# A decode step of attention: values as the 512-wide moving operand in six groups in place of two, and output weights on the lowest eight DMA engines

## The chip, the cores and the metric

The kernel runs on one core of a Trainium2 chip. A core has TensorE (matrix products, written to PSUM), VectorE, ScalarE, GpSimdE and SyncE, and 16 DMA engines that carry data from HBM to SBUF, the on-chip memory of 128 partitions. The engines run on their own and meet at semaphores. The metric is the device time of the kernel in microseconds; the profile's span is that of one profiled execution, from its first to its last instruction.

## What is computed

One token goes through attention with 32 heads of 128 values over the last 4096 positions of a cache, beside a small gated network; the two are multiplied and added to the input. Cut to what matters:

```python
xn = layernorm(A_x)                                  # 1 x 512
q  = (xn @ A_wq).reshape(32, 128)
k, v = A_k_cache[:, 32768-4096:], A_v_cache[:, 32768-4096:]      # per head 4096 x 128
p  = softmax(q @ k.T * 128**-0.5)                    # per head 1 x 4096
o  = (p @ v).reshape(1, 4096)                        # all heads side by side
s  = o @ A_wo                                        # 1 x 512
h  = gelu(layernorm(xn + mix(gelu(layernorm(xn) @ B_w1)) @ B_w2) @ B_w3) @ B_w4
out = A_x + s * silu(xn + mix(...) @ B_w2 + h)
```

With one position, the shifted mix of the small network is zero. K and V are 32 MB each of bf16, and each number is used once. The matrix w4 has 1376 rows (ten blocks of 128, and 96), wo has 4096 rows.

## The kernel before

**Groups and stages.** The 32 heads are worked in 8 groups of 4. A group's K is one tile of 128 partitions by 128 columns by 128 values (4 MB): each head has 32 partitions, and each column holds one position of each partition. V is the same. A loop of ten stages runs K two groups ahead of V (`LAG = 2`): stage s scores the keys of group s, takes the softmax of group s-1, and multiplies the values of group h = s-2. TensorE, VectorE and ScalarE work in exactly the written order (a manual schedule); a wait of one instruction holds all that is behind it on its engine.

**Scores.** Of the 128 columns, `nd(g)` go to VectorE, in four parts of a product and a sum (L308, L310): 64 columns in groups 0, 1 and 7, 68 in group 3, 80 in the others. The rest go to TensorE in batches of up to 8: a transpose (L324), a copy by ScalarE (L326), a product with q (L332). `keys(b0, b1)` does some of these batches.

**Softmax.** `sm_max` (VectorE) takes the maximum per partition, `sm_turn` turns it on TensorE (L354) and VectorE takes the maximum per head (L356), `sm_exp` spreads it (L363) and takes four exponentials on ScalarE (L370). `sm_den` (L376) adds up the sums, and `sm_rden` (L381) takes the reciprocal on VectorE.

**Values**, `v_part`. In the ordinary form (L430) each of the 128 columns of V is the stationary operand, and the four probabilities of the column are the moving one: 128 weight loads and 128 narrow products, which give the 4 heads as columns. In the form for groups in `MOVED` (L422) the probabilities of four columns are the stationary operand (16 wide), and four columns of V, 512 numbers, the moving one: 32 loads and 32 wide products, which give 16 by 512 numbers. Only the blocks where the two column numbers agree are wanted. ScalarE copies them to SBUF (L425), and `v_add` (L437) adds the four blocks with selected columns of the identity: 4 float32 products, which the machine runs as 8. `v_add` and `v_out` of a group in `MOVED` are in the next stage, behind `sm_den` and `sm_rden`; for the others `v_out` (L453, for the last two groups L449) follows at once. The results of `sm_den`, `v_add`, `sm_turn` and `sm_exp` share one PSUM buffer, so each waits until the one before it has been read.

**The output product.** wo is used in three blocks: heads 0 to 15 (`wo0`, by the wide product L496 in stage 6), heads 16 to 23 (stage 8), and heads 24 to 31. In the last, heads that finish early are spread to partitions by `ox_spread`, `ox_pick` and `ox_few`, so that one group of 32 small products covers several heads (`y_block`, L150), and the remaining ones go head by head (`y_head`). `NE` says over how many DMA engines this block's early rows, the tile `wo_few`, are laid out: `FEW = 64 * NE` rows. With `NE = 5` these are 320 rows, heads 24, 25 and half of 26. Its load has two parts, each with an outer dimension of `NE`. The other rows come as `wo_rows`: half of head 26 and head 27 ahead of the last V, heads 28 to 31 behind it.

**Loads.** SyncE issues all the big loads (L79) in one order, as written, each when its buffer is free: K has three buffers (one of them later holds wo), V has two. So V of a group is issued when the values two groups before are done. The last V comes in cuts of 64, 48 and 16 columns, and TensorE multiplies each as it lands.

Of the kernel before, what the change touches and what calls it, by code (L numbers as in the profile page):

```python
# [8 lines left out]
P = 128  # L9
# [9 lines left out]
G = 4  # L19
LAG = 2  # L20
K_BUFS = 3
NE = 5
V_BUFS = 2
EARLY = 2
LATE = 7
MOVED = (0, 2)


@with_exitstack
def kernel(  # L30
# [14 lines left out]
    nc = tc.nc  # L45
# [3 lines left out]
    _, H, Sk, Dh = A_k_cache.shape  # L49
# [8 lines left out]
    F = B_w3.shape[1]  # L58
# [19 lines left out]
    def load(dst, src):  # L78
        return tc.keep_in_program_order(nc.sync.dma_start(out=dst, in_=src))  # L79
# [9 lines left out]
    load(w3_sb[:], B_w3.rearrange("(p c) n -> p c n", p=P))  # L89
    w4_sb = wts.tile([P, 11, D], BF16, name="w4_sb")  # L90
    load(w4_sb[:, 0:10, :], B_w4[0:10 * P, :].rearrange("(p c) n -> p c n", p=P))
    load(w4_sb[0:96, 10, :], B_w4[10 * P:F, :])
    wq_sb = wts.tile([P, KC, HD], BF16, name="wq_sb")

    load(wq_sb[:].rearrange("p c n -> p (c n)"), A_wq.rearrange("(a b c) n -> b a (c n)", a=2, c=KC))
# [51 lines left out]
    def rows_add(ps, col, w, last):  # L147
        k = col.shape[0]
        for j in range(KC):
            nc.tensor.matmul(ps[32 * j:32 * j + 1, :], lhsT=col, rhs=w[0:k, j * P:(j + 1) * P],  # L150
                             start=False, stop=last, skip_group_check=True)
# [114 lines left out]
    for c in range(2):  # L266
        nc.vector.tensor_copy(
            out=few[:, c, 0:4 * NE].rearrange("p (a b) -> p a b", b=4),
            in_=ident_bf[:, 4 * NE * c:4 * NE * (c + 1)].rearrange("p (b a) -> p a b", b=4))

# [79 lines left out]
    def sm_turn(g):  # L350

        s = st[g]
        mt_ps = ps_misc.tile([1, P], FP32, tag="misc", name="mt_ps")
        nc.tensor.transpose(mt_ps[:], s["m1"][:], ident_f[:])  # L354
        mx = sm_pool.tile([1, G], FP32, tag="mx", name="mx")
        nc.vector.tensor_reduce(out=mx[:], in_=mt_ps[:].rearrange("r (b a) -> r a b", a=G), axis=AX.X,  # L356
                                op=ALU.max)
        nc.vector.tensor_scalar(out=md[0:1, :], in0=mx[:], scalar1=-scale, scalar2=None, op0=ALU.mult)
# [28 lines left out]
    few_h = blocks[few_block][0]  # L387
    FEW = 8 * 8 * NE
    h_part = few_h + FEW // P

    r_part = FEW % P
    o_blk, wo_blk, ox_blk = {}, {}, {}

    def load_wo(i):
        h0, n = blocks[i]
        load(wo_blk[i], A_wo[h0 * P:(h0 + n) * P, :].rearrange("(p t) n -> p t n", p=P))

    def load_few():
        t = wo_blk[few_block]
        for c in range(2):  # L400
            r0 = few_h * P + c * FEW // 2
            load(t[32 * c:32 * c + 4 * NE],
                 A_wo[r0:r0 + FEW // 2, :].rearrange("(b a t) n -> a b (t n)", b=4, a=NE))

    def wo_row(h):
        return wo_rows[:, h - h_part, :]

    def load_rows(h, n):
        if h == h_part:
            load(wo_rows[r_part:P, 0, :], A_wo[h * P + r_part:(h + 1) * P, :])  # L410
            h, n = h + 1, n - 1
        load(wo_rows[:, h - h_part:h - h_part + n, :],
             A_wo[h * P:(h + n) * P, :].rearrange("(h p) n -> p h n", p=P))

# [2 lines left out]
    def v_part(g, v, c0=0, c1=CP):  # L417
        s = st[g]
        if g in MOVED:
            s["ov"] = ps_o.tile([4 * G, 4, Dh], FP32, tag="oT", name="ov")  # L420
# [12 lines left out]
    def v_add(g):  # L433
        s = st[g]
        s["oT"] = ps_misc.tile([P, G], FP32, tag="misc", name="oT")
        for j in range(4):
            nc.tensor.matmul(s["oT"][:], lhsT=s["ov_sb"][:, j, :], rhs=ident_f[0:4 * G, G * j:G * j + G],  # L437
                             start=(j == 0), stop=(j == 3))

    def v_out(g):  # L440
        h = G * g
        b = [i for i, (h0, _) in enumerate(blocks) if h >= h0][-1]
        if b not in o_blk:
            o_blk[b] = sm_pool.tile([P, blocks[b][1]], BF16, tag=f"o{b}", bufs=1, name="o")
            if b == few_block:
                nc.gpsimd.memset(o_blk[b][:], 0.0)
        c = h - blocks[b][0]
        if g >= NG - 2:
            nc.vector.tensor_tensor(out=o_blk[b][:, c:c + G], in0=st[g]["oT"][:], in1=st[g]["rden"][:],  # L449
                                    op=ALU.mult)  # L450
            return
        for k in range(G):
            nc.scalar.mul(o_blk[b][:, c + k:c + k + 1], st[g]["oT"][:, k:k + 1], st[g]["rden"][:, k:k + 1])  # L453


    def ox_spread(i):
        n = blocks[i][1]
        to, mt, mh = masks[n]
        spread = sm_pool.tile([P, n, n], BF16, tag=f"spread{n}", bufs=1, name="spread")
        nc.vector.tensor_tensor(out=spread[:], in0=o_blk[i][:].unsqueeze(2).to_broadcast([P, n, n]),  # L460
                                in1=mt[:].unsqueeze(1).to_broadcast([P, n, n]), op=ALU.mult)
        ox_blk[i] = spread
# [42 lines left out]
    def y_head(h):  # L505
        rows_add(y_ps, o_blk[few_block][:, h - few_h:h - few_h + 1], wo_row(h), h == H - 1)
# [7 lines left out]
    for s in range(NG + LAG):  # L514
        h = s - LAG
        last = h == NG - 1
        kn = load_kv(k_pool, A_k_cache, s, (0, 64, CP) if s == 0 else (0, CP)) if s < NG else None
        if s == LAG:
            wts_guard.__exit__(None, None, None)
            v_pool = ctx.enter_context(tc.tile_pool(name="v", bufs=V_BUFS))  # L520
            wo_blk[few_block] = v_pool.tile([64, 8, D], BF16, tag="wo_few", bufs=1, name="wo_few")
            nc.gpsimd.memset(wo_blk[few_block][:], 0.0)
            wo_rows = v_pool.tile([P, H - h_part, D], BF16, tag="wo_rows", bufs=1, name="wo_rows")
            nc.gpsimd.memset(wo_rows[0:r_part, 0, :], 0.0)
        if last:
            load_rows(h_part, 2)
            v = load_kv(v_pool, A_v_cache, h, cuts)
            for r, n in ((H - G, 2), (H - 2, 1), (H - 1, 1)):
                load_rows(r, n)
        elif h >= 0:  # L530
            v = load_kv(v_pool, A_v_cache, h)
        if h == 3:
            wo_24 = k_pool.tile([P, 32, D], BF16, tag="kv", name="wo_24")
            wo_blk[0], wo_blk[1] = wo_24[:, 0:16, :], wo_24[:, 16:24, :]
            load_wo(0)
        if h == 5:
            load_wo(1)
            load_few()

        if s < NG:  # L540
            nb = len(batches(s))

            def keys(b0, b1):
                for b in range(b0, b1):
                    k_turn(s, kn, b)
                    if b > 0:
                        k_scores(s, b - 1)

            k_open(s)
            k_vector(s, kn, 0)  # L550
            keys(0, 2)
            if s > 1:
                sm_den(s - 2)
                sm_rden(s - 2)
            if h - 1 in MOVED:
                v_add(h - 1)
                v_out(h - 1)
            keys(2, 4)
            k_vector(s, kn, 1)
            if s > 0:  # L560
                sm_turn(s - 1)
            if s == 6:
                ox_spread(0)
            keys(4, nb)
            k_scores(s, nb - 1)
            sm_own(s)
            if s > 0:
                sm_exp(s - 1)
            k_vector(s, kn, 2)
            if s == 6:  # L570
                ox_pick(0)
            k_vector(s, kn, 3)
            if h >= 0:
                v_part(h, v)
            sm_max(s)
            if s == 6:
                y_wide(0, 0, 16)
            if h >= 0 and h not in MOVED:
                v_out(h)
        elif s == NG:  # L580

            sm_den(NG - 2)
            sm_rden(NG - 2)
            sm_turn(NG - 1)
            ox_spread(1)
            sm_exp(NG - 1)
            ox_pick(1)
            y_block(1)
            rows_add(y_ps, one_f, y_row, False)
            v_part(h, v)  # L590
            v_out(h)
            ox_spread(few_block)
            sm_den(NG - 1)
            sm_rden(NG - 1)
            ox_pick(few_block)
            ox_few(few_block)
        else:
            v_part(h, v, 0, cuts[1])
            y_block(few_block)
            for r in range(h_part, H - G):  # L600
                y_head(r)
            for c0, c1 in zip(cuts[1:], cuts[2:]):
                v_part(h, v, c0, c1)
            v_out(h)
            for r in range(H - G, H):
                y_head(r)
# [36 lines left out]
```

## Time and profile before

The median of three timed runs is 195.14 us (194.98 to 195.44), the profiled span 193.2 us.

| engine | busy us | share of the span |
|---|---|---|
| PE (TensorE products) | 132.6 | 69% |
| PEld (weight loads, beside the products) | 102.3 | 53% |
| DVE (VectorE) | 143.8 | 74% |
| ACT (ScalarE) | 87.1 | 45% |
| all loads | 78.84 MB read | mean 408 GB/s |

The page gives for each engine its busy share in 40 slices of the span (4.83 us each) as a digit in tenths, and below it the granted TensorE clock, the busy share of the DMA engines, and the rate. A timeline line has the start and the length in us, the engine, the line of the kernel, the operation, what is written and read, and how many instructions were merged; in brackets stands how long the engine was idle before, and what ended that. Where the reason is "issue", the engine waited for nothing that the profile shows.

### The profile page before, as it was taken

The numbers are of one execution on the slowest core, as the hardware profiler recorded it, in microseconds if no ns is written. First come the engines' busy times: TensorE is split into PE (matmuls) and PEld (weight loads), VectorE is DVE, ScalarE is ACT, GpSimd is POOL, SyncE is SP. The second block draws the span as 40 slices with busy tenths as digits, with TensorE's granted clock in tenths as the row PEclk, the third lists the DMA queues.
The fourth block names the chain that finished last, engine by engine and source line by source line (L and its number), as shares of the span: only waits on it lengthen the run. The fifth ranks groups of instructions, "written<-read, shape, count | busy, mean of one in ns | idle before, by whom it ended". The sixth has DMA issues, their size and how long they took to land.

```text
span 193.2 us, 4769 instructions
## 1 busy us (share of the span) xinstructions
PE 132.6 (69%) x2123; PEld 102.3 (53%) x2123; DVE 143.8 (74%) x162; ACT 87.1 (45%) x195; POOL 6.4 (3%) x14
## 2 busy tenths in 40 slices
PE   0549763977736579798898938840878879845792
PEld 0444463866625433486884428740768257733771
DVE  0560208999999999999999999990899999931201
ACT  2003002888896360468568044731574077813000
POOL 2110008000000000000000000000000000000000
PEclk9999955588755557978559995855576696755555
DMA  6999999999999999999999999999999999999980
GB/s 205 417 472 427 397 427 453 421 427 424 434 431 434 434 433 421 434 427 434 424 431 434 431 434 407 461 431 434 431 427 426 427 424 407 458 417 377 416 326 8
DMA packets 4725, 79.13 MB, mean 410 GB/s; under 512 B 666, under 2 KB 1466, under 8 KB 1722
## 3 DMA queue, kind: packets, MB, share of 16 engines
q1 hardware_dynamic: 4554, 78.84, 96.0%
q8 instruction: 16, 0.26, 0.5%
q10 hardware_dynamic: 152, 0.00, 0.0%
q14 instruction: 3, 0.02, 0.0%
HBM read 78.84 MB, written 0.00 MB: 408 GB/s over the span
## 4 chain that ended last, share of the span: by engine, by line
DVE 50%; DMA 24%; PE 16%; issue 5%; ACT 3%; POOL 1%; SPq 0%; ACTq 0%; POOLq 0%
DVE S L310 29%; DVE prod L308 16%; DMA kv<-in_A_k_cache_dram 14%; DMA kv<-in_A_v_cache_dram 8%; PE oT L430 3%; PE yr_ps L496 3%; ACT kt L326 2%; DMA x_bf<-in_A_x_dram 2%; PE qT_ps L244 2%; PE hr_ps L228 2%; PE a_ps L217 1%; PE pt L324 1%; PE hr_ps L225 1%; PE sT L332 1%; DVE S L346 1%
## 5 line engine op out<-in xcount | busy, mean ns | idle before, releaser
L310 DVE TENSOR_REDUCE S<-prod 128x20 f32<-128x2560 bf16 (+2 forms) x32 | 82.2, 2570 | 1.1
L326 ACT COPY kt<-pt 128x1024 bf16<-128x1024 bf16 (+1 forms) x56 | 54.5, 1007 | 20.9 <-PE pt L324 20.3
L324 PE MATMUL pt<-ident_bf,kv 128*128 128x128 bf16 x444 | 47.1, 276 | 7.1 <-DMA kv<-in_A_k_cache_dram 7.1
L308 DVE TENSOR_TENSOR prod<-kv,q_bc 128x2560 bf16<-128x2560 bf16 (+2 forms) x32 | 43.5, 1360 | 7.6 <-DMA kv<-in_A_k_cache_dram 4.9
L324 PEld LDWEIGHTS <-kv 128*128 128x128 bf16 x444 | 38.0, 127 | 9.2 <-DMA kv<-in_A_k_cache_dram 7.9
L332 PE MATMUL sT<-qT_bf,kt 128*128 128x4 bf16 x444 | 20.6, 168 | 16.9 <-ACT kt L326 16.3
L332 PEld LDWEIGHTS <-kt 128*128 128x128 bf16 x444 | 17.1, 103 | 24.5 <-ACT kt L326 24.1
L430 PE MATMUL oT<-pT,kv 128*128 128x4 bf16 x768 | 21.8, 166 | 7.6 <-issue 5.5
L430 PEld LDWEIGHTS <-kv 128*128 128x128 bf16 x768 | 21.1, 103 | 9.6 <-issue 5.7
L422 PE MATMUL ov<-kv,pT 128*16 128x512 bf16 x64 | 16.6, 425 | 0.0
L370 ACT ACTIVATE pT<-S,mb 128x128 bf16<-128x128 f32 x32 | 13.9, 570 | 0.3
L453 ACT ACTIVATE o<-oT,rden 128x1 bf16<-128x1 f32 x24 | 4.3, 261 | 15.5 <-PE oT L430 9.0
L422 PEld LDWEIGHTS <-pT 128*16 128x16 bf16 x64 | 6.1, 98 | 9.5 <-issue 3.5
L449 DVE TENSOR_TENSOR o<-oT,rden 128x4 bf16<-128x4 f32 x2 | 0.3, 162 | 12.4 <-PE oT L430 12.4
L341 ACT ACTIVATE own<-sT,par 128x48 f32<-128x48 f32 (+2 forms) x32 | 7.6, 361 | 3.6 <-PE sT L332 3.1
L370 ACT ACTIVATION_READ_ACCUMULATOR pT<-S,mb 128x1 f32 x32 | 8.2, 255 | 0.0
L231 DVE COPY hr<-hr_ps 1x512 f32<-1x512 f32 x1 | 0.7, 679 | 8.3 <-PE hr_ps L228 8.3
L425 ACT COPY ov_sb<-ov 16x512 f32<-16x512 f32 x2 | 1.1, 575 | 12.1 <-PE ov L422 12.1
L437 PE MATMUL oT<-ident_f,ov_sb 16*128 16x4 f32 x16 | 2.9, 301 | 4.1 <-DVE rden L381 4.1
L496 PE MATMUL yr_ps<-wo,ox 128*1 128x512 bf16 x16 | 4.9, 476 | 1.2 <-DVE ox L474 1.2
L220 ACT ACTIVATE a_bf<-a_ps 128x10 bf16<-128x10 f32 x1 | 0.2, 179 | 12.1 <-PE a_ps L217 12.1
L354 PE MATMUL mt_ps<-ident_f,m 128*1 128x128 f32 x8 | 2.8, 354 | 3.3 <-DVE rden L381 3.3
(117 smaller groups left out, 92.0 us busy)
## 6 DMA issues: line engine op xcount, KB each, us to landing
kv<-in_A_k_cache_dram SPq DMA_DIRECT2D x7, 4096.0 KB, 29.4
kv<-in_A_v_cache_dram SPq DMA_DIRECT2D x7, 4096.0 KB, 33.8
wq_sb<-in_A_wq_dram SPq DMA_DIRECT2D x1, 4096.0 KB, 18.4
kv<-in_A_k_cache_dram SPq DMA_DIRECT2D x2, 2048.0 KB, 22.6
wo<-in_A_wo_dram SPq DMA_DIRECT2D x1, 2048.0 KB
kv<-in_A_v_cache_dram SPq DMA_DIRECT2D x1, 2048.0 KB, 11.9
kv<-in_A_v_cache_dram SPq DMA_DIRECT2D x1, 1536.0 KB, 15.0
w_sb<-in_B_w_dram SPq DMA_DIRECT2D x1, 1376.0 KB
```

The source lines that it names most:

```text
L228: nc.tensor.matmul(hr_ps[:], lhsT=a_bf[0:m, i:i + 1], rhs=w4_sb[0:m, i, :], start=False, stop=(i == len(chunks) - 1))
L308: nc.vector.tensor_tensor(out=prod[:, 0:m, :], in0=kn[:, rows, :], in1=q_bc[:, g:g + 1, :].to_broadcast([P, m, Dh]), op=ALU.mult)
L310: nc.vector.tensor_reduce(out=st[g]["S"][:, rows], in_=prod[:, 0:m, :], axis=AX.X, op=ALU.add)
L324: nc.tensor.transpose(pt[:, c - c0, :], kn[:, c, :], ident_bf[:])
L326: nc.scalar.copy(out=kts[b][:, 0:c1 - c0, :], in_=pt[:, 0:c1 - c0, :])
L332: nc.tensor.matmul(st[g]["sT"][:, c - nd(g), :], lhsT=kt[:, c - c0, :], rhs=qT_bf[:, G * g:G * g + G], start=True, stop=True)
L341: nc.scalar.mul(s["own"][:, 0:m, a], s["sT"][:, 0:m, a], par[:, a:a + 1])
L370: nc.scalar.activation(out=s["pT"][:, :, a], in_=s["S"][:], func=ACT.Exp, scale=scale, bias=mb[:, a:a + 1], accum_out=s["sum"][:, a:a + 1])
L422: nc.tensor.matmul(s["ov"][:], lhsT=s["pT"][:, c:c + 4, :].rearrange("p i a -> p (i a)"), rhs=v[:, c:c + 4, :], start=(c == 0), stop=(c == ...
L430: nc.tensor.matmul(s["oT"][:], lhsT=v[:, c, :], rhs=s["pT"][:, c, :], start=(c == 0), stop=(c == CP - 1))
L453: nc.scalar.mul(o_blk[b][:, c + k:c + k + 1], st[g]["oT"][:, k:k + 1], st[g]["rden"][:, k:k + 1])
L496: nc.tensor.matmul(yr[i][:], lhsT=ox_blk[i][:, t:t + 1], rhs=wo_blk[i][:, t, :], start=(t == 0), stop=(t == n - 1))
```

## The change

Two things are changed together. First, `NE` goes from 5 to 8: `wo_few` takes 512 rows of wo, heads 24 to 27, with an outer dimension of 8, and the 96 last rows of w4 are read with an outer dimension of 8 as well. The loads of the rows of heads 26 and 27 and their `y_head` fall away. It is for levelling the DMA engines[...]. Second, `MOVED` goes from groups 0 and 2 to groups 0 to 5, so that four more groups take the wide form of the values, which has fewer TensorE instructions. As group 5 is now among them, its `v_add` and `v_out` come in stage 8.

```diff
-NE = 5
+NE = 8
-MOVED = (0, 2)
+MOVED = (0, 1, 2, 3, 4, 5)
...
-    load(w4_sb[0:96, 10, :], B_w4[10 * P:F, :])
+    load(w4_sb[0:96, 10, :], B_w4[10 * P:F, :].rearrange("(a b) n -> a b n", a=8))
...
     def load_rows(h, n):
-        if h == h_part:
-            load(wo_rows[r_part:P, 0, :], A_wo[h * P + r_part:(h + 1) * P, :])
-            h, n = h + 1, n - 1
...
         if last:
-            load_rows(h_part, 2)
             v = load_kv(v_pool, A_v_cache, h, cuts)
...
             sm_turn(NG - 1)
+            if h - 1 in MOVED:
+                v_add(h - 1)
+                v_out(h - 1)
             ox_spread(1)
...
             y_block(few_block)
-            for r in range(h_part, H - G):
-                y_head(r)
```

More of the change, by code (lines that the diff above doesn't have):

```diff
@@ L389 @@
     h_part = few_h + FEW // P
-    r_part = FEW % P
+    assert FEW % P == 0 and h_part == H - G
     o_blk, wo_blk, ox_blk = {}, {}, {}
@@ L523 @@
             wo_rows = v_pool.tile([P, H - h_part, D], BF16, tag="wo_rows", bufs=1, name="wo_rows")
-            nc.gpsimd.memset(wo_rows[0:r_part, 0, :], 0.0)
         if last:
-            load_rows(h_part, 2)
             v = load_kv(v_pool, A_v_cache, h, cuts)
```

## The prediction

> **What bounds the kernel now.** I read the page from the top: the rates over the span first, then the chain that ended last, then the timeline of TensorE and of SyncE's queue where the two meet.
>
> ```profile
> DVE  0560208999999999999999999990899999931201
> PEclk9999955588755557978559995855576696755555
> DMA  6999999999999999999999999999999999999980
> ...
> q8 instruction: 16, 0.26, 0.5%
> ```
>
> The DMA row is at 9 from the second slice to the third from the end, and windows from 78 to 171 us all move 429 to 433 GB/s. So the 78.8 MB set the end, but only as long as the next load is always issued before the last one runs out. The clock row shows TensorE mostly between half and full speed. The queue q8, which fetches instructions, took 16 packets.
>
> The issue that is tightest is V of group 7, the last big load. V has two buffers, so this load must wait until TensorE has read V of group 5 (L430):
>
> ```profile
> 166.07 3.43 PE L430 MATMUL oT<-pT,kv 128*128 128x4 bf16 x124
> 171.05 0.27 PE L430 MATMUL oT<-pT,kv 128*128 128x4 bf16 x4 [1.55 <-issue]
> 171.18 0.57 PE L376 MATMUL den_ps<-sum,ones_f 128*128 128x4 f32 x2
> ```
>
> ```profile
> 171.35 1.86 SPq L79 DMA_DIRECT2D kv<-in_A_v_cache_dram  x3
> 173.25 5.01 SPq L79 DMA_DIRECT2D wo_rows<-in_A_wo_dram  x3
> 190.46 0.61 SPq L79 DMA_DIRECT2D out_dram<-out_row  x1
> ```
>
> Call T the moment when TensorE ends V of group 5: now 171.32. The trace's packet records have the first packet of the last V at 173.46, straight behind the wo rows queued before it: 2.1 us of reserve, no more. From T to the end of the span are 21.9 us, a chain of softmax, two output products and the head rows. Of these, few are waits for loads (1.7 us before V of group 6, 0.2 before the second cut of V 7). So TensorE's own work has about two microseconds to spare at the end.
>
> The values operation exists in both forms:
>
> ```profile
> 103.89 7.07 PE L422 MATMUL ov<-kv,pT 128*16 128x512 bf16 x32
> 110.90 1.07 PE L324 MATMUL pt<-ident_bf,kv 128*128 128x128 bf16 x16
> 112.62 0.35 PE L332 MATMUL sT<-qT_bf,kt 128*128 128x4 bf16 x8 [0.66 <-ACT kt L326]
> 112.84 0.36 PE L376 MATMUL den_ps<-sum,ones_f 128*128 128x4 f32 x2
> 116.56 1.86 PE L437 MATMUL oT<-ident_f,ov_sb 16*128 16x4 f32 x8 [3.35 <-DVE rden L381]
> ```
>
> Here group 2 took 7.07 us as a moving operand (group 0: 9.54), where group 4 took 3.53 as a stationary one. And the fold (L437) stands in TensorE's queue until VectorE's rden (L381), which is queued behind a 4.3 us score part, so the transposes behind it start late.
>
> [...]about 427 ns apart at the start of group 0, 7.07/32 = 221 in group 2. [...]L430 waits 5.5 us in three places for "issue", up to 3.25 us, when such a packet comes late. [...]The trace has no engine numbers, but 5 landings of each wo_few half.
>
> **The change part by part.** *Loads.* One DMA engine moves 430/16 = 27 KB per us. [...]The 16 landings of the last wo row were spread from 185.6 to 189.4, which is what this levels. The latest could move by 0.2 to 0.7 us if nothing else did: this is the prize. The w4 piece lands near 11.7 us and is read near 20, so its cost is nothing.
>
> *Instructions.* Groups 1, 3, 4, 5 go from 256 to 64 TensorE instructions and get 16 for the fold: 704 fewer. The heads of y_head(26) and (27) go too, 16 more, but wo_few covers them in the same 32 matmuls. [...]13 fetches for 16. Gaps of 1.05 us and packets slower by 0.47 us in the records put one fetch at 1.5 us on its engine, so K of group 6 may land up to 1.5 us earlier.
>
> *TensorE.* Each new group costs 7.07 (full clock) to 9.54 us for 3.5, plus a stall of 0 to 3.25 that goes, and its fold 1.05 to 1.86 us plus the wait for rden. [...]I take the full-clock value for most and half of the difference as the upper side. I lay the stages end to end from measured pieces.
> Stage 3: values of group 1 start at 90.6 as now, end 97.7 (now 95.0).
> Stage 4: transposes 2.8 us later, den, rden at 100.8, fold to 102, remaining keys 6.2 us, values of group 2 at 108.5, end 115.6 (now 110.96).
> Stage 5: VectorE is 2.6 us late too, rden at 119.2, fold to 120.3, keys 6.3, values of group 3 at 126.6, end 133.7 to 135 (now 131.4). Here K of group 6 lands at 135.7 (or 134.2), and VectorE now idles 4.9 us: nearly all the lateness is absorbed.
> Stage 6: from 135.7. den as now at 138.7, but the fold waits for rden at 140.1 and ends at 141.2; keys 6.3, exp and pick 1.0: values of group 4 at 148.5 (now 145.7), end 155.5 (now 149.2). Then the wide product of block 0 (L496), 3.5 (full clock) to 4.9 us: 159.0 to 160.5 (now 155.3). K of group 7 is long there, so this is 3.7 us or more lost.
> Stage 7: den +2.8, rden +0.2, fold +1.05, keys 8.2: values of group 5 at 171.3 (now 166.1), + 7.07 = 178.4.
> So T goes from 171.3 to about 178.4. No slack stands behind it: V of group 7 is issued 7 us late and finds its engines idle, for V 6 is in by 177.9.
>
> *After T.* Loads: first packet T + 1.0 (as the first load of the kernel), two cuts of 224 KB per engine in 8.5 us, 0.3 to land, 1.5 for a fetch: T + 11.3 for the second cut. TensorE: it gains a fold of group 5 ahead of the exponent of group 7, because they share one PSUM buffer: mx at T + 1.4, fold 1.05, outputs 0.8, against now: about +1.8. So values of group 6 start at T + 6.7 (now T + 6.6 with 1.7 of waiting). Then 5.4 to the first cut, 3.1 to the second (heads 26 and 27 are out): T + 15.2. The loads are ready 4 us before that, so TensorE sets the end. From the second cut to the end now 6.25. Sum: T + 21.4 = 199.8 us of span. The timed run lies 195.14 - 193.2 = 1.9 above the span: 201.7.
>
> **The rivals.** *Half clock:* every new piece at its slow value, group 3 ends at 136.9, group 4 at 160, the wide product at 165, T near 187.7, and 22.2 after it: 211.8. The clock row's many 5s speak for it, the full clock in group 2 and at the end of group 0 against it; a mix gives 205 to 207. *Partly absorbed:* an earlier K 6 (1.5 us), full-clock keys in stages 6 and 7 and no fetch stalls bring T to 174.5; 174.5 + 21.4 + 1.9 = 197.8. It needs most pieces to go well at once. *Hidden, and the levelling counts (the other side):* TensorE's idle time takes up the wider products, T stays below 173.5, and the loads still set the end, 0.2 to 0.7 us earlier: 194.6. For it speaks that TensorE is busy 69% of the span; against it that stage 6 is 16.5 of 19.4 us busy already and gets some 6 more. *The last V sets the end:* T + 11.3 + 6.25 is 4 us less than TensorE's chain, so it doesn't make a time of its own.
>
> **How the numbers follow.** TensorE late, T from 176.5 to 182: 0.70, giving 201.7. Half clock or a mix above 206.5: 0.10. Partly absorbed: 0.11. Hidden: 0.09, of which a third is no change. The range runs from just above the partly absorbed case, 198, to 206.5. Faster 0.06, same 0.03, slower 0.91.
>
> **What would show it.** Values at L418 (the new line of L422) in groups 4 and 5 ending near 155.5 and 178; the SyncE issue of the last V moving from 171.35 to there; the DMA row, 9 until now, with a hole at 174 to 179 us; 13 packets on q8; K 7 no longer what the transposes of stage 7 wait for. I am wrong if that issue stays before 174, or if the DMA row has no hole. If T is right but the end is not, the chain after T was mis-sized: then look whether the last values wait for loads.

## The result, and the profile after

The changed kernel takes 203.88 us (median; 203.0 to 205.82) where the kernel before took 195.28 us beside it: a ratio of 1.0456, with a 95% interval of 1.0401 to 1.0511. It is slower by about 8.6 us. The profiled span is 201.2 us, 8.0 more than the 193.2 of before; it is that of the fastest of the four executions (203.0 us).

The page's rows over the span, the queue that fetches instructions, and the chain that ended last:

```profile
DMA  6999999999999999999999999999999999919970
GB/s 196 427 426 371 397 423 451 443 430 420 417 427 449 430 435 430 423 423 446 430 423 433 443 394 453 433 430 430 446 432 417 443 383 461 417 42 313 378 254 3
q8 instruction: 14, 0.23, 0.5%
PE 37%; DVE 29%; DMA 16%; ACT 13%; issue 2%; ACTq 0%
L418 PE MATMUL ov<-kv,pT 128*16 128x512 bf16 x192 | 53.0, 445 | 0.0
```

The DMA row has one new thing, the 1 in its 36th slice. A slice is 201.2/40 = 5.03 us, so the hole lies at 176 to 181 us, and there the rate falls to 42 GB/s. Before, the row was at 9 up to there. TensorE now leads the chain with 37%, where VectorE had 50% and TensorE 16%. The last line says what the wide values cost: 53.0 us for 6 groups of 32, or 276 ns for a product.

Where the hole comes from is seen in the timeline of TensorE (start, length, what it did, how many instructions; in brackets the idle time before):

```profile
91.94 8.76 PE L418 MATMUL ov<-kv,pT 128*16 128x512 bf16 x32
...
110.37 8.42 PE L418 MATMUL ov<-kv,pT 128*16 128x512 bf16 x32
...
128.64 9.51 PE L418 MATMUL ov<-kv,pT 128*16 128x512 bf16 x32
...
148.62 9.76 PE L418 MATMUL ov<-kv,pT 128*16 128x512 bf16 x32
158.21 3.62 PE L492 MATMUL yr_ps<-wo,ox 128*1 128x512 bf16 x16
...
164.34 1.05 PE L433 MATMUL oT<-ident_f,ov_sb 16*128 16x4 f32 x8 [0.27 <-DVE rden L381]
...
173.25 7.08 PE L418 MATMUL ov<-kv,pT 128*16 128x512 bf16 x32
```

and in that of SyncE's queue:

```profile
180.36 1.86 SPq L79 DMA_DIRECT2D kv<-in_A_v_cache_dram  x3
```

The reader is to see one number in both. TensorE ends V of group 5 at 173.25 + 7.08 = 180.33 us (T), and the last V is issued at 180.36; before, these were 171.32 and 171.35. T has moved by 9.0 us and the end of the span by 8.0.

How TensorE's clock stood in these pieces is in the windows (stretch, its length, busy time and count of PE, PEld, DVE, ACT and POOL, then granted clock, DMA share and GB/s). These four are the keys of stage 6 with the fold, the values of group 4, the keys of stage 7, and the values of group 5:

```profile
138.10:148.60 10.50, 7.76 (x111) 6.67 (x110) 9.87 (x9) 8.26 (x17) 0.00 (x0) 0.77 1.01 432
148.60:158.20 9.60, 9.60 (x33) 3.45 (x33) 8.85 (x9) 1.43 (x8) 0.00 (x0) 0.71 1.01 434
161.80:173.20 11.40, 9.06 (x142) 7.86 (x141) 8.92 (x9) 9.11 (x14) 0.00 (x0) 0.85 0.99 424
173.20:180.30 7.10, 7.10 (x35) 2.87 (x34) 2.53 (x3) 2.58 (x13) 0.00 (x0) 1.00 0.44 187
```

Group 4's values took 9.76 us at a granted clock of 0.71, group 5's 7.08 us at 1.00. In the last window the loads move only 187 GB/s: this is where the DMA engines run dry. The hole shows that TensorE is late; whether it also makes the end late is a question of its own, answered below.

### The profile page after: what moved, and what is told of

Same layout as the page of the kernel before. It is cut to its first block, busy times and chain, and to the rows that moved or that the text cites. A ratio compares the mean times of both kernels' runs of the same rounds, so it can differ in the third digit from the quotient of the medians.

```text
span 201.2 us, 4052 instructions
## 1 busy us (share of the span) xinstructions
PE 155.9 (77%) x1763; PEld 103.8 (52%) x1763; DVE 144.0 (72%) x162; ACT 89.5 (44%) x199; POOL 6.0 (3%) x13
## 4 chain that ended last, share of the span: by engine, by line
PE 37%; DVE 29%; DMA 16%; ACT 13%; issue 2%; ACTq 0%
PE ov L418 17%; DVE S L310 17%; DMA kv<-in_A_k_cache_dram 14%; ACT kt L326 10%; DVE prod L308 9%; PE pt L324 5%; PE oT L426 4%; PE sT L332 3%; PE oT L433 3%; DMA x_bf<-in_A_x_dram 2%; ACT o L449 2%; PE yr_ps L492 2%; PE y_ps L150 2%; ACT own L341 1%; PE mb_ps L363 1%
## 5 line engine op out<-in xcount | busy, mean ns | idle before, releaser
L418 PE MATMUL ov<-kv,pT 128*16 128x512 bf16 x192 | 53.0, 445 | 0.0
L324 PE MATMUL pt<-ident_bf,kv 128*128 128x128 bf16 x444 | 46.6, 274 | 3.5 <-DMA kv<-in_A_k_cache_dram 3.5
L324 PEld LDWEIGHTS <-kv 128*128 128x128 bf16 x444 | 36.9, 124 | 6.3 <-DMA kv<-in_A_k_cache_dram 3.7
L418 PEld LDWEIGHTS <-pT 128*16 128x16 bf16 x192 | 19.1, 102 | 31.7 <-issue 15.5
L421 ACT COPY ov_sb<-ov 16x512 f32<-16x512 f32 x6 | 3.4, 574 | 40.0 <-PE ov L418 40.0
L381 DVE RECIPROCAL rden<-den_ps 128x4 f32<-128x4 f32 x8 | 1.4, 178 | 13.3 <-PE den_ps L376 13.3
L433 PE MATMUL oT<-ident_f,ov_sb 16*128 16x4 f32 x48 | 6.3, 250 | 2.5 <-DVE rden L381 2.1
L426 PEld LDWEIGHTS <-kv 128*128 128x128 bf16 x256 | 7.1, 104 | 1.9 <-issue 1.9
L426 PE MATMUL oT<-pT,kv 128*128 128x4 bf16 x256 | 7.5, 166 | 0.5 <-issue 0.5
L433 PEld LDWEIGHTS oT<-ident_f,ov_sb 16*128 16x128 f32 x48 | 5.8, 186 | 3.1 <-DVE rden L381 2.5
L220 ACT ACTIVATE a_bf<-a_ps 128x10 bf16<-128x10 f32 x1 | 0.2, 179 | 12.3 <-PE a_ps L217 12.3
## 6 DMA issues: line engine op xcount, KB each, us to landing
wq_sb<-in_A_wq_dram SPq DMA_DIRECT2D x1, 4096.0 KB, 19.7
```

Of the source, the lines that this page charges most:

```text
L324: nc.tensor.transpose(pt[:, c - c0, :], kn[:, c, :], ident_bf[:])
L418: nc.tensor.matmul(s["ov"][:], lhsT=s["pT"][:, c:c + 4, :].rearrange("p i a -> p (i a)"), rhs=v[:, c:c + 4, :], start=(c == 0), stop=(c == ...
L426: nc.tensor.matmul(s["oT"][:], lhsT=v[:, c, :], rhs=s["pT"][:, c, :], start=(c == 0), stop=(c == CP - 1))
```

## The experiments

Eleven kernels were run, each timed beside the kernel before. The questions were: is it the values or the loads; which groups; what of the loss lies ahead of T and what behind; and what in TensorE's own order can give it back.

**Each half of the change alone.** The first kernel has the values of the change and the loads of before, the second the loads of the change and the values of before. The third is the second with the last rows of w4 read as before.

```diff
e1_values_only, against before
-MOVED = (0, 2)
+MOVED = (0, 1, 2, 3, 4, 5)
+            if h - 1 in MOVED:
+                v_add(h - 1)
+                v_out(h - 1)
...
e2_loads_only, against after
-MOVED = (0, 1, 2, 3, 4, 5)
+MOVED = (0, 2)
...
e3_loads_w4_even, against e2_loads_only
-    load(w4_sb[0:96, 10, :], B_w4[10 * P:F, :].rearrange("(a b) n -> a b n", a=8))
+    load(w4_sb[0:96, 10, :], B_w4[10 * P:F, :])
```

> The kernel before with the wide form of the values in groups 0 to 5, and the loads as before. If TensorE's lateness is the cause (theory A): nearly all of the loss is here, 202 to 205 us, the last V issued near 180 in place of 171.4, and a hole in the DMA row. If the loads[...] are the cause (theory B): 194.5 to 196 us. If it is the late issue of the last V and the idle DMA engines behind it (theory C): the same 202 to 205, so this run tells A and C from B, and not from each other.

> The changed loads[...], with the wide values in groups 0 and 2 only. Theory A: 194.4 to 195.2 us, the 16 landings of the last wo row closer together than the 3.9 us of before. If the w4 piece is what made the load of wq take 1.2 us longer in the changed kernel: 196.0 to 196.5. Theory B: 198 us or more.

> As the run with the changed loads only[...]. If the w4 piece slows the load of wq behind it: 1.0 to 1.3 us below the run with both, and wq lands near 21 us as before. If that slowness has nothing to do with w4: the same as the run with both within 0.3 us. Against before: 194.4 to 195.0 if levelling wo_few helps[...], and heads 26 and 27 are no work of their own.

Measured: values alone 203.66 us, ratio 1.0393 (1.034 to 1.0447). Loads alone 195.48, ratio 1.0028 (1.0012 to 1.0045). Without the w4 piece 195.53, ratio 1.0032 (1.0016 to 1.0049). The values carry the loss, as expected; the hoped-for gain of the loads (194.4 to 195.2, and 194.4 to 195.0 without the w4 piece) did not come. In the first kernel, profiled in an execution of 204.68 us, T is 172.69 + 8.70 = 181.39 and the last V is issued at 181.42:

```profile
172.69 8.70 PE L422 MATMUL ov<-kv,pT 128*16 128x512 bf16 x32
```

The loads bring nothing; they cost 0.3%, and the w4 piece has no part in it. Where the levelling went is seen in the waits for V in the second kernel:

```profile
179.00 3.58 PE L426 MATMUL oT<-pT,kv 128*128 128x4 bf16 x128 [2.94 <-DMA kv<-in_A_v_cache_dram]
...
184.20 1.86 PE L426 MATMUL oT<-pT,kv 128*128 128x4 bf16 x64
...
187.48 1.87 PE L426 MATMUL oT<-pT,kv 128*128 128x4 bf16 x64
```

V of group 6 is waited for 2.94 us, where it was 1.73 before. The rows of heads 26 and 27 used to be queued behind V 6; now they lie ahead of it, in `wo_few` (each of its two loads has 5 landings in the profile of before and 8 in that of the change). But this order alone is not the cost: the third kernel has the same order, and there the wait for V 6 is 1.17 us, less than before.

In the landing records of the second kernel the last wo row lands earlier on most engines than before (median 187.5 against 188.4 us), but two of its 16 landings come at 189.93 and 189.98. So the landings are spread over 5.1 us instead of 3.9, where they were expected closer together. In the third kernel one lands late, at 190.17, and the last cut of V is waited for 0.97 us. What makes these landings late, and so what the 0.3% are, isn't shown, as the records do not say which engine a packet is of.

**Which groups.** The next four kernels change only `MOVED`: groups 0 to 3 with the loads of the change, the same with the loads of before, then the change without group 5 and without group 4.

```diff
e4_first_four, against after
-MOVED = (0, 1, 2, 3, 4, 5)
+MOVED = (0, 1, 2, 3)
...
e8_before_first_four, against before
-MOVED = (0, 2)
+MOVED = (0, 1, 2, 3)
...
e6_without_5, against after
-MOVED = (0, 1, 2, 3, 4, 5)
+MOVED = (0, 1, 2, 3, 4)
...
e7_without_4, against after
-MOVED = (0, 1, 2, 3, 4, 5)
+MOVED = (0, 1, 2, 3, 5)
```

> The changed kernel with the wide values in groups 0 to 3 only, 4 and 5 as before. Theory A: the idle time before K of group 6 takes up most of what groups 1 and 3 lose; the last V is issued at 173 to 176 and the time is 195.5 to 198 us, a quarter or less of the loss. If each of the four groups costs the same: half of the loss, 199.5 us.

> The kernel before with the wide form in groups 0 to 3 and the loads as before. With the changed loads this form came out at 1.0009 of before and the loads alone at 1.003, so if the two add up this is 0.1 to 0.3% faster than before, 194.6 to 195.1 us, by one or two instruction fetches fewer. If the fetches don't set the end: the same as before.

> The changed kernel with the wide form in groups 0 to 4. Theory A: group 5 costs 3.5 us more in the wide form, less a fetch stall of 0 to 2, and its fold 1.8 us after that; so 3.3 to 5.3 us less than the changed kernel, 198.5 to 200.5. Theory C: the issue alone moves, 2 to 3.5 us less.

> The changed kernel with the wide form in groups 0, 1, 2, 3 and 5. Theory A: group 4's product is 6 us shorter (9.8 to 3.6), but the wide product of block 0 then waits for VectorE's ox at 150.3 or later, and the fold of group 4 in stage 7 goes: T comes 4 to 7 us earlier, 197 to 199.5 us. If only the last wide group counts: no gain, 203.

| kernel | T, us | profiled span, us | time, us | ratio (95%) |
|---|---|---|---|---|
| before | 171.32 | 193.2 | 195.28 | 1 |
| groups 0 to 3 | 171.16 | 193.5 | 195.54 | 1.0009 (0.9993 to 1.0025) |
| groups 0 to 3, loads of before | 172.73 | 194.3 | 195.23 | 0.9992 (0.9968 to 1.0016) |
| change without group 5 | 175.03 | 196.2 | 199.39 | 1.0189 (1.0136 to 1.0242) |
| change without group 4 | 176.05 | 197.9 | 199.89 | 1.0158 (1.0074 to 1.0241) |
| the change | 180.33 | 201.2 | 203.88 | 1.0456 (1.0401 to 1.0511) |

Groups 1 and 3 are free within the intervals, and their 176 instructions fewer in each (192, less 16 for the fold) bring no time either. Of the expectations, those for groups 0 to 3 (in time; the last V was issued at 171.19, not late as expected) and for the change without group 5 came true; with the loads of before the time was that of before, not less; the change without group 4 came out 0.4 us above its range, with T 4.3 us earlier, as forecast. Before, TensorE waited 4.21 us for K 6 and began stage 6 at 135.72. With groups 0 to 3 it begins at 136.98, without that wait; the values of group 5 then run without the stall of 1.55 us that they had, and T is where it was. With the loads of before it begins at 138.54 and T is 1.4 us later. That profile is of an execution of 196.1 us, 0.9 above the median, and its loads ran late from the start (wq took 19.5 us, against 18.3 with the changed loads), so the 1.4 us are not put down to the edit. In the kernel with groups 0 to 3 the loads still set the end:

```profile
167.59 3.57 PE L426 MATMUL oT<-pT,kv 128*128 128x4 bf16 x128
177.32 3.58 PE L426 MATMUL oT<-pT,kv 128*128 128x4 bf16 x128 [1.05 <-DMA kv<-in_A_v_cache_dram]
182.53 1.87 PE L426 MATMUL oT<-pT,kv 128*128 128x4 bf16 x64
187.35 1.87 PE L426 MATMUL oT<-pT,kv 128*128 128x4 bf16 x64 [2.01 <-DMA kv<-in_A_v_cache_dram]
```

Against groups 0 to 3 (195.54), group 4 added costs 3.9 us, group 5 added 4.4, and both 8.3: within the scatter of four runs each they add, as both stand behind the last place that absorbs. In the table the span is T + 20.9 to T + 22.3 in every row: the end follows T.

**The loads behind T.** This kernel is the change without the load of the last V: the values of group 7 are taken from the V of group 6, so its output is another one.

```diff
e5_no_last_v, against after
-            v = load_kv(v_pool, A_v_cache, h, cuts)
```

> The changed kernel without the load of V of group 7: its last product reads V of group 6 again, so 4 MB of 78.8 are left out and the last group's values are those of group 6. Nothing is then late on the DMA engines. Theory A (TensorE's own chain after the values of group 5 sets the end): within 1.5 us of the changed kernel, 202 to 204.5. Theory C (the late issue of the last V sets it): 3 us or more faster, below 200.5.

Measured: 201.6 us (200.14 to 203.7), ratio 1.0283 (1.0222 to 1.0344). It lies between the two expectations, and neither is borne out as written. T is 180.96 in its profile, so nothing ahead of T has changed, and from T to the end are 19.3 us instead of 20.9. Part of the 1.6 us is in the first cut; in the change it is in two pieces:

```profile
191.62 1.26 PE L426 MATMUL oT<-pT,kv 128*128 128x4 bf16 x41
193.41 0.77 PE L426 MATMUL oT<-pT,kv 128*128 128x4 bf16 x23 [0.54 <-issue]
...
195.07 1.87 PE L426 MATMUL oT<-pT,kv 128*128 128x4 bf16 x64
```

and without the last V in one:

```profile
191.66 1.86 PE L426 MATMUL oT<-pT,kv 128*128 128x4 bf16 x64
194.40 1.86 PE L426 MATMUL oT<-pT,kv 128*128 128x4 bf16 x64
```

TensorE doesn't wait for the data of the last V in the change: the first cut starts 11.3 us after T, behind TensorE's own work, and 10.7 us after T without the load. So 0.6 of the 1.6 us lie ahead of this cut, where the products of one output block took 1.02 us instead of 0.62 and the small ones behind it 0.60 instead of 0.42; 0.7 lie in the cut, most of it the 0.54 us without instructions ("issue"); the rest lies behind the second cut. That the load is the reason for this pause is not shown, with one profile of each kernel. The rest of the difference between the medians, 2.3 us less these 1.6, is within what such kernels scatter. So the last V carries some 2 us of the 8.6 at most, and the rest is TensorE's own lateness.

**What gives it back.** Two edits shorten TensorE's work ahead of T. One makes the fold in bf16, which rounds that part more coarsely. The other gives 16 more columns of group 7 to VectorE, 80 for 64, since it idles 4.37 us for rden in stage 7 (`nd(g)` is 64 for the groups from `LATE` on).

```diff
e9_fold_bf16, against after
-            s["ov_sb"] = sm_pool.tile([4 * G, 4, Dh], FP32, tag="ov_sb", bufs=1, name="ov_sb")
+            s["ov_sb"] = sm_pool.tile([4 * G, 4, Dh], BF16, tag="ov_sb", bufs=1, name="ov_sb")
...
-            nc.tensor.matmul(s["oT"][:], lhsT=s["ov_sb"][:, j, :], rhs=ident_f[0:4 * G, G * j:G * j + G],
+            nc.tensor.matmul(s["oT"][:], lhsT=s["ov_sb"][:, j, :], rhs=ident_bf[0:4 * G, G * j:G * j + G],
...
e10_sixteen_more_keys, against after
-LATE = 7
+LATE = 8
...
e11_both: the two edits together
```

> This kernel rounds the four blocks of the wide values to bf16 before the fold (L433), so that part is computed with less precision; all else is the changed kernel. Theory (TensorE's own order of work carries the lateness): a fold takes 1.05 us in float32 (8 instructions for 4 products); in bf16 I expect about 0.3. Folds stand in TensorE's path in stages 4, 5, 6, 7 and once behind T: T 1.4 to 2.5 us earlier than 180.3, and 0.7 behind it: 200.5 to 202 us against 203.9. Rival (the length of the wide products scatters with the clock and hides it): the fold is shorter, T is not, 202.5 to 204.

> VectorE takes 80 columns of group 7 in place of 64, so TensorE has 16 fewer to transpose and multiply in stage 7, where VectorE idles 4.4 us for rden. Theory (in stage 7 TensorE is the one that is late, VectorE has room): some 2 us less of keys on TensorE, T about 2 us earlier, 201.5 to 202.5 us against 203.9. Rival (VectorE becomes the late one, as group 7's maximum comes behind its longer score part): T no more than 0.5 us earlier or the exponent of group 7 later, 203.5 to 205.

> The two edits above together, the fold in bf16 (less precise in that part) and 16 more columns of group 7 on VectorE. If both lie on TensorE's path ahead of T they add: 198.5 to 200.5 us, still slower than the kernel before (195.3). If only one counts, 201 to 203.

Measured: the bf16 fold 197.94 us (196.23 to 201.18), ratio 1.0135 (1.0082 to 1.0188). More keys on VectorE 202.88 (201.37 to 205.68), ratio 1.0402 (1.0361 to 1.0444). Both 199.14 (198.42 to 199.8), ratio 1.0216 (1.0183 to 1.0249). The first expectation missed, as the fold gave more than I thought. The second missed both its ranges, and the kernel can't be told from the change. The third lies in its range, but not for its reason: the two don't add, since the fold alone is at 197.94.

The fold itself is as expected, 0.23 us as 4 instructions where the float32 one took 1.05 as 8. From the timeline and the windows of the kernel with the bf16 fold (stage 6 keys, values of group 4, stage 7 keys, values of group 5):

```profile
138.45 0.23 PE L433 MATMUL oT<-ident_bf,ov_sb 16*128 16x4 bf16 x4 [0.35 <-DVE rden L381]
...
167.27 7.07 PE L418 MATMUL ov<-kv,pT 128*16 128x512 bf16 x32
```

```profile
135.80:145.00 9.20, 6.05 (x107) 5.04 (x107) 9.10 (x9) 8.10 (x17) 0.00 (x0) 1.00 0.99 426
145.00:153.60 8.60, 8.60 (x33) 3.24 (x33) 8.32 (x7) 1.50 (x8) 0.00 (x0) 0.80 1.01 435
157.20:167.20 10.00, 7.30 (x138) 6.14 (x137) 8.47 (x9) 9.00 (x14) 0.00 (x0) 1.00 0.99 421
167.20:174.30 7.10, 7.10 (x35) 2.88 (x34) 3.90 (x4) 2.59 (x13) 0.00 (x0) 1.00 0.99 422
```

T is 167.27 + 7.07 = 174.34, 6.0 us earlier than in the change. Stage 6 begins at 135.79 instead of 138.08 (2.3 us), its keys and fold take 9.2 instead of 10.5, the values of group 4 8.75 instead of 9.76, stage 7's keys and fold 10.1 instead of 11.5. Each fold explains 0.82 of these; the rest goes with the clock, which stood at 1.00 in three of the four windows, where in the change it was 0.77, 0.85 and 1.00. Of the 2.3 us about one may not be the fold's: the kernel with more keys on VectorE, whose fold is as in the change, began stage 6 at 137.11. The medians of the two kernels are 5.9 us apart, so the 6.0 us are not an accident of these two profiles. Whether the shorter fold brings the better clock isn't shown, as each kernel has one profile. With TensorE this much earlier, the loads count again: the second cut of the last V is waited for 0.78 us.

The other edit shows the opposite. In its profile:

```profile
170.89 9.99 PE L418 MATMUL ov<-kv,pT 128*16 128x512 bf16 x32
```

Stage 7 up to the values got shorter, from 11.5 to 9.8 us, and the wide product behind them longer, 9.99 us for 7.08, at a granted clock of 0.70. T is 180.88. VectorE, which my rival blamed, isn't the reason: rden is waited for 0.28 us, as in the change (0.27). The kernel with both edits has the same, 10.01 us for group 5, and T at 176.17.

## Why the prediction was right

**What sets the end.** Right. The chain was: the last V is issued when TensorE ends V of group 5, TensorE falls behind from stage 6 on, and all of it goes to the end. The hole in the DMA row came (42 GB/s at 176 to 181 us, forecast 174 to 179, as T was forecast 2 us earlier), the issue moved with T to within 0.03 us, and over all rows of the table the span follows T. As forecast, it is TensorE's own chain behind T that ends last, not the late load: without that load at all, 6.3 of the 8.6 us remain.

**T = 178.4.** Too early by 1.9 us; it was 180.33. The step that was off is "I take the full-clock value for most": 7.07 us for a group, my estimate from group 2 alone. Measured were 8.76, 8.42, 9.51, 9.76 and 7.08. What groups 1 to 3 took too long was absorbed almost whole, so what reached T is group 4's excess. The row of the values in the profile of before held the better figure: 16.6 us busy for 64 products is 8.3 us a group, the mean of its two groups. I had taken the lower of the two instead. The wide product of block 0, in turn, was at its full-clock value (3.62 us at a granted clock of 1.00, forecast 3.5 to 4.9).

**What stages 3 to 5 cost.** Right for the time: the kernels with groups 0 to 3 are at 0.9992 and 1.0009. But the lateness was absorbed only in part by the wait for K 6. VectorE began on K 6 at 135.55 in the change, while TensorE began its keys only at 138.08, since group 3 took 9.51 us; the forecast had it begin at 135.7. These 2.4 us cost only about half a microsecond, because the fold waits for rden, and rden stands on VectorE behind the score part that began with K 6:

```profile
135.55 1.49 DVE L308 TENSOR_TENSOR prod<-kv,q_bc 128x2560 bf16<-128x2560 bf16 x1 [0.36 <-DMA kv<-in_A_k_cache_dram]
137.07 2.82 DVE L310 TENSOR_REDUCE S<-prod 128x20 f32<-128x2560 bf16 x1
140.42 0.18 DVE L381 RECIPROCAL rden<-den_ps 128x4 f32<-128x4 f32 x1 [0.53 <-PE den_ps L376]
```

It came at 140.42, with 140.1 in the forecast. VectorE was done with the score part at 139.89 and then idled 0.53 us for TensorE's den (L376): that is the part of the lateness that came through.

**Stages 6 and 7.** 148.62 for the start of group 4 (forecast 148.5), 173.25 for that of group 5 (171.3). The rden waits were 0.27 to 0.34 us, 0.2 in the forecast, and the folds 1.05. Stage 7 took 11.5 us up to the values; the pieces of the forecast add up to 12.3 from the wide product's end at 159.0. What made T late is group 4 alone, 9.76 us for 7.0, less the 0.8 that stage 7 was shorter; group 5 took its full-clock 7.08.

**T + 21.4.** It was T + 20.9. TensorE set this, not the last V, as the rival "the last V sets the end" also had it: the two cuts landed by T + 7.7 and T + 13.2, TensorE began them at T + 11.3 and T + 14.7. But the reserve there was 1.5 us, where the forecast had 4: it had the second cut at T + 11.3. And some 1.6 us of the chain go when the last V isn't loaded, a cost that the prediction did not have. That the sum still came out is in part luck: the stretches up to the values of group 6, to the first cut and behind the second were 0.6, 0.2 and 0.1 us shorter than I had laid them, the one between the cuts 0.35 longer. T too early and the rest too long also cancel in part.

**The loads' prize, 0.2 to 0.7 us.** Wrong in sign, and small: +0.3% alone. The prize was my estimate, from sums of the bytes on each engine, and which engines a load lies on was not shown. The records show only how many landings a load has: each half of `wo_few` 5 before and 8 in the change, the last rows of w4 16 in both. With the changed loads alone the landings of the last wo row lay further apart than before (5.1 us for 3.9). Why the sign came out wrong stays open. In the forecast of the time it played no part, since TensorE sets the end there.

**13 fetches.** It was 14 (16 before), for 4052 instructions in the profile instead of 4769. That 13 would do was my estimate; how many instructions a fetch brings was not shown. K of group 6 was to land up to 1.5 us earlier, at 134.2; it came at 135.55. In the same profile the load of wq, at the start, took 19.7 us against 18.4 before. With the bf16 fold and 13 fetches wq took 18.3 and K 6 came at 133.97, in line with the step where wq isn't late. Why wq was late stays open: it was at 19.5 to 19.7 in the change, in the values alone and in groups 0 to 3 with the loads of before, and at 18.1 to 18.4 in all others where the profile has it, with no edit that the three share and the others lack. It may belong to the single execution rather than to the kernel; with one profile of each, that can't be told.

**The rivals.** Half clock throughout (211.8) would need 9.54 us in every group and slower keys; four of the five new or old wide products behind stage 2 were at 8.4 to 9.8, so it was nearer than I had it: T at 180.33 lies between 178.4 and the 187.7 of that case. "Hidden" is what the kernels with groups 0 to 3 do, but at 195.2 to 195.5, without the gain to 194.6.

**The clock.** In the clock records of the profiles of before and of the change, from 20 us on, the granted clock is 0.50 or 1.00, in stretches of 3.41 to 51.20 us. The instructions of a wide product stand about 427 ns apart where it is 0.50 and about 216 where it is 1.00. The eight wide products of values in these two profiles follow one sum to within 0.05 us: 7.07 us, and half of the time that the product spent at half clock, which is 2.76 to 5.47 us in six of the eight and none in the other two. Over all 13 profiles six of the 60 took 7.07 or 7.08 us, the others 8.26 to 10.01, and the mean is 9.04; so the full-clock value that the forecast took is the exception. Two of the 60 are group 4 of the change (lines 1 and 2) and group 5 with 16 more columns on VectorE (lines 3 and 4); the third number from the end is the granted clock:

```profile
148.60:154.10 5.50, 5.50 (x14) 1.75 (x14) 5.43 (x5) 1.43 (x8) 0.00 (x0) 0.50 0.99 425
154.10:158.20 4.10, 4.10 (x20) 1.70 (x19) 3.41 (x5) 0.00 (x0) 0.00 (x0) 1.00 1.04 448
170.90:176.80 5.90, 5.90 (x15) 1.87 (x15) 5.83 (x4) 2.24 (x12) 0.00 (x0) 0.50 0.64 278
176.80:180.80 4.00, 4.00 (x19) 1.54 (x17) 0.57 (x3) 0.00 (x0) 0.00 (x0) 1.00 0.00 0
```

Both begin at half clock and end at full clock. This also tells why the 16 columns brought nothing in their profile: in stage 7 of the change a stretch of 3.41 us at half clock ended at 171.15, before the product; with the 16 columns the clock stood at 0.50 until about 176.8 and took in 5.9 us of the product (the third line). Half of that is 2.95 us, and the product took 2.92 us more than 7.07. Why the clock fell there earlier and stayed low longer, no experiment shows. Nor is it shown that the clock makes the scatter of the kernels with five or six wide groups: 203.0 to 205.82 in four runs of the change, 196.23 to 201.18 in six with the bf16 fold, where 96 runs of the kernel before lie within 194.32 to 197.77. Only one execution of each kernel has a trace, and the mean clocks of the others don't order their times (0.739 at 203.0 us, 0.755 at 205.82).

No version beat the kernel before. The ones that come level (groups 0 to 3) take out TensorE instructions where TensorE isn't late.

## What to carry to other kernels

An operand order with a quarter of the instructions (32 products for 128) was no gain here where the data rate set the end (groups 0 to 3: 195.54 and 195.23 us for 195.28), and became a loss as soon as its longer streaming time (7.07 to 10.01 us for 3.5) stood on the path of the engine that ends last (3.9 us for group 4, 4.4 for group 5): find the last place that absorbs lateness (here the start of stage 6, at K 6 and rden) and count only what stands behind it. A load that is issued late is a sign of this lateness and need not be what it costs (here some 2 of 8.6 us at most); leave the load out to see. For the length of a long dense product take the mean of all its occurrences, busy time over count (8.3 us here before), not its best one (7.07). The loads that were to level the DMA engines brought no gain (+0.3%): look at the 16 landings of the last load for the one that is late (189.98 with the changed loads alone, where the median is 187.5).

## What the hardware showed beside that

- Before, the first 13 packets of q8 (16 KB each, the last at 168.50 us) took 1.00 to 1.11 us. With 12 of them, 15 packets of the loads were under way in the middle of such a packet, and 16 just ahead of it and just behind; the 32 KB packet of a load that began as it ended took 1.68 to 1.76 us, where 1.21 is usual. By these figures one fetch holds one DMA engine for about 1.5 us, an estimate.
- In the first cut of the change TensorE stood idle for 0.54 us with the reason "issue" (until 193.41), and a packet of q8 had run from 191.22 to 192.19; in the profile without the last load the same products ran in one piece. That the products waited for this fetch is not shown.
- After the hole in the change, the first 16 packets of 16 KB of the last V took 1.35 to 1.72 us, where 0.61 us is usual in the running stream. By these figures the restart costs about a microsecond beside the idle time, an estimate.
- Four float32 products (16x128 by 16x4) run as 8 instructions and take 1.05 us; the same four in bf16 take 0.23.
